# Weight scaling, low parts and partition copies moved to VectorE, q and k loaded ahead of the cap, and a new order, in an attention and gated-MLP kernel

## The chip, the cores and the metric

The kernel runs on one core of a Trainium2 chip. The metric is device time in microseconds: 728.2 us, the median of three runs (727.88 to 729.52). TensorE does the matrix products, VectorE (DVE), ScalarE (ACT) and GpSimd (POOL) the elementwise work, and SyncE (SP) issues the transfers.

## The reference, cut to what matters

```python
B, H, S, D = 8, 12, 448, 64                      # attention; DM = H*D = 768
scores = q @ k.T / sqrt(D);  scores = cap * tanh(scores / cap)
attn = exp(scores - max);    attn = attn / (attn.sum(-1) + 1e-9)
x = (attn @ v), heads joined to (B, S, 768)
h = relu(x @ w_in)                                # 768 x 1024
u, v = h[..., :512], h[..., 512:]
v_n = (v - mean(v)) / sqrt(var(v) + 1e-6)
v_s = w_spatial @ v_n (over the sequence) + b_spatial
out = (u * v_s) @ w_out                           # 512 x 768
```

All is float32; w_in and w_out come as float64 (the kernel reads their bits as pairs of 32-bit words).

## The kernel before, in words

The program has two variants behind a branch on the cap's value; with the cap of 30 the bounded one runs (`quad_bnd`, `moe`). In it no maximum is subtracted ahead of the exponential: exp(cap*tanh) is summed as it is, and the maximum enters only with the small constant of the denominator.

Attention goes in 24 turns (`quad_bnd`), three a batch, each of four heads. In a turn seven blocks of 64 keys are worked on. For each, TensorE makes the scores (L594), ScalarE the tanh out of PSUM (L598), then, over pairs of blocks, the exp (L605), and TensorE multiplies with v (L615). VectorE folds the exp tiles over the blocks for the maximum and, from the fourth turn on, for the sum (L633), transposes and reduces (L641, L643). In the first three turns TensorE makes the sums instead, by matmuls with ones (L662). Then the denominators: two copies between groups of 32 partitions (L649, tile `sh`), a join of both halves (L652, L679), in the first three turns DMAs that bring the sums to the tile `dt` (L674), a transpose, a reciprocal (L685), a round trip through DRAM that spreads the reciprocals over the partitions (L686, L689), and the multiplication (L698). `halves` splits the result into a rounded part and its rest, in the tile `xg`.

The MLP of a batch (`moe`) follows when its six `xg` tiles are there: chains of matmuls for u and v, the norm of v, the spatial product (L845 to L850) with the gate, and the output product. Each product takes three matmuls, high by high, high by low and low by high parts. So the weights have to be split once, in the first part of the program: `split_f64` for w_in (twelve pieces of 512 columns) and w_out (twelve of 256) takes six passes: a scaling (L420), three integer passes (L424, L425, L427), a rounding (L355) and the rest (L351), with the engines of the first, fifth and sixth in `E_W`. `split_f32` does w_spatial in four pieces, the last with the bias in two rows of the low part.

The order of all this is made when the program is built. `Plan.order` is a planner: it runs the tasks on a model of the engines, with the durations that each `add` names, and takes on each engine the ready task with the smallest key. The keys are made from `BND_KEY` and `BND_ADJ`, per kind and turn, and `BND_W_KEYS` for the weights. Buffers of one tag are also given in the order of the keys. `TURN` is what the planner charges when TensorE changes between the attention's and the MLP's kinds of matmul. Each engine then works in order, waiting on semaphores. The first MLP unit has `FILL` matmuls of weights by weights ahead of it, whose product is overwritten, and the program begins with `WARM` matmuls of zeros while the cap and the first q and k are loaded; the branch is decided by the cap, which all engines read.

Of the kernel before, what the change touches and what calls it, by code (L numbers as in the profile page):

```python
# [21 lines left out]
QB = 14  # L22
# [20 lines left out]
class Plan:  # L43
# [8 lines left out]
    TURN, STICK = 180.0, 5.6142  # L52
# [131 lines left out]
HW, HH, XL = 400, 620, 50  # L184
# [19 lines left out]
def dve(n):  # L204
    return 1.06 * n + 70
# [10 lines left out]
def gpc(n):  # L216
# [4 lines left out]
LATE = ("vh", "vl", "o")  # L221
# [4 lines left out]
    "xg": (XW, F32R, 8), "u": (448, F32, U_LEAD), "vh": (512, F32R, 4), "vl": (512, F32R, 4),  # L226
# [19 lines left out]
BND_KEY = dict(ld=20.2062, vld=16.3748, sc=-4.4101, th=2.6266, ex=-12.5751, pv=3.8334, sm=4.9568, mx=1.2536,  # L246
               dn=-1.9573, ev=0.5509, x=0.5743, moe=3.5126, span=11.5964, step=-1.1271, mv=-7.699, vld_=0.5863, sc_=0.1716,
               th_=0.234, ex_=3.1048, pv_=-0.3915, sm_=-0.1418, mx_=1.5249)
BND_ADJ = dict(sc0=-1.9208, sc1=-0.6751, sc2=-0.5665, sc3=0.6591, sc4=1.0022, sc5=0.9243, sc6=0.5641, sc7=3.5286,
               sc8=4.1291, sc9=2.1364, sc10=0.4432, sc11=-0.3562, sc21=1.0782, sc22=-2.0787, sc23=-1.8651, mx0=7.5468, mx1=4.1712,  # L250
               mx2=0.2306, mx3=-3.4986, mx4=-4.2501, mx5=-7.8699, mx6=-6.59, mx7=-4.2274, mx8=-1.6152, mx9=-1.0965, mx10=-2.503,
               mx11=2.4712, mx21=3.6487, mx22=7.5152, mx23=10.1101, sm0=-23.9232, sm1=-5.9121, sm2=-19.3382, sm3=-4.1068,
               sm4=-7.6692, sm5=-6.9113, sm6=-7.6076, sm7=-2.9296, sm8=-4.8786, sm9=-2.9017, sm10=0.1476, sm11=-1.028,
               sm21=7.8004, sm22=5.003, sm23=9.0892, dn0=-13.9326, dn1=2.5665, dn2=1.5054, dn3=3.678, dn4=5.4586, dn5=2.0101,
               dn6=-0.9345, dn7=1.341, dn8=5.2032, dn9=5.9753, dn10=6.5428, dn11=-0.3824, dn21=0.2627, dn22=-7.9155, dn23=32.9005,
               x0=-1.8155, x1=-12.9607, x2=-3.0392, x3=-3.3476, x4=1.7459, x5=0.4945, x6=3.9029, x7=6.1809, x8=0.3782, x9=6.0115,
# [698 lines left out]
```

## Time and profile before

| | |
|---|---|
| median of the runs | 728.2 us |
| profiled execution, its own time (given as the span alone) | 726.5 us |
| PE busy | 713.2 us (98%) |
| DVE busy | 600.4 us (83%) |
| ACT busy | 479.9 us (66%) |
| POOL busy | 78.4 us (11%) |

The page shows busy time by engine and, in forty slices, when it falls. A busy TensorE is not TensorE at its peak, since its matmuls overlap and their ends are modelled; the distance from one start to the next says more. The chain that ended last is 79% TensorE and 12% VectorE. Idle time of an engine that is not the bound costs nothing.

### The profile page before, as it was taken

To read this page: it belongs to the slowest core of one execution; us is meant where nothing else is said; L and a number is where in the kernel's file an instruction comes from. 1 tells how busy PE (TensorE), PEld (TensorE's weight loads), DVE (VectorE), ACT (ScalarE), POOL (GpSimd) and SP (SyncE) were. 2 spreads that over 40 slices of the span, in tenths; PEclk is the share of its full clock that TensorE was granted. 3 is DMA by queue.
4 is the path that set the end of the run, shared out by engine and by line. 5 is a ranking of instruction groups with operands and counts; after the bars stand their busy time and mean duration, and the time that the engine had idled before them with its cause. 6 is when DMAs were issued, how large, how long until landed. Compare 5 with 4: busy or idle time off the path is not lost.

```text
span 726.5 us, 12274 instructions
## 1 busy us (share of the span) xinstructions
PE 713.2 (98%) x4910; PEld 487.7 (67%) x4910; DVE 600.4 (83%) x849; ACT 479.9 (66%) x648; POOL 78.4 (11%) x71
## 2 busy tenths in 40 slices
PE   8998999999999999999999999999999999999997
PEld 3333576575668657785568688568566865699896
DVE  4899999999999989948999996299799778983520
ACT  6999757849883894649875833786876678424321
POOL 1234310600110001000120001000021000200100
PEclk9999999999999999999999999999999999999999
DMA  8564314524221431033321430124321131202002
GB/s 279 165 204 148 129 38 134 168 80 142 85 78 30 149 129 49 28 91 114 102 76 28 153 103 27 49 66 141 102 77 41 47 131 39 53 2 101 1 1 80
DMA packets 34263, 66.50 MB, mean 92 GB/s; under 512 B 6034, under 2 KB 21908, under 8 KB 34196
## 3 DMA queue, kind: packets, MB, share of 16 engines
q1 hardware_dynamic: 34196, 65.62, 28.3%
q8 instruction: 40, 0.66, 0.4%
q14 instruction: 27, 0.22, 0.1%
HBM read 54.40 MB, written 11.18 MB: 90 GB/s over the span
## 4 chain that ended last, share of the span: by engine, by line
PE 79%; DVE 12%; issue 4%; ACT 2%; DMA 1%; SPq 1%; POOL 0%; DVEq 0%; ACTq 0%; POOLq 0%
PE ps_s L594 13%; PE ps_x L615 13%; PE ps_acc L870 5%; PE ps_acc L871 5%; PE ps_acc L872 5%; PE ps_acc L754 4%; PE ps_acc L756 4%; PE ps_acc L755 4%; DVE red L633 4%; PE ps_acc L779 4%; PE ps_acc L780 3%; PE ps_acc L781 3%; PE ps_acc L848 2%; PE ps_acc L850 2%; PE ps_acc L849 2%
## 5 line engine op out<-in xcount | busy, mean ns | idle before, releaser
L598 ACT ACTIVATE tp<-ps_s,capt 128x896 f32<-128x896 f32 x168 | 162.2, 1003 | 28.6 <-PE ps_s L594 18.1
L633 DVE TENSOR_TENSOR red<-red,tp 128x1792 f32<-128x1792 f32 x90 | 140.9, 1566 | 22.5 <-ACT tp L605 20.8
L605 ACT ACTIVATE tp<-tp,capt 128x1792 f32<-128x1792 f32 (+1 forms) x96 | 154.0, 1606 | 1.5
L594 PE MATMUL ps_s<-raw 64*64 64x448 f32 x1344 | 147.1, 545 | 3.6 <-ACT tp L598 3.5
L615 PE MATMUL ps_x<-tp,v 64*64 64x448 f32 x1344 | 140.0, 536 | 0.5 <-ACT tp L605 0.4
L633 DVE TENSOR_TENSOR red<-tp 128x1792 f32<-128x1792 f32 x45 | 91.2, 2027 | 13.9 <-ACT tp L605 13.0
L615 PEld LDWEIGHTS ps_x<-tp,v 64*64 64x64 f32 x1344 | 51.3, 133 | 75.7 <-issue 68.2
L594 PEld LDWEIGHTS ps_s<-raw 64*64 64x64 f32 x1344 | 47.1, 132 | 80.1 <-issue 46.5
L803 POOL TENSOR_TENSOR lst<-lst,capt 128x1 f32<-128x1 f32 x32 | 34.9, 1091 | 526.7 <-DVE lst L801 482.9
L754 PE MATMUL ps_acc<-xg,wi_h 128*128 128x448 f32 x180 | 66.2, 368 | 0.5 <-ACT xg L355 0.5
L755 PE MATMUL ps_acc<-xg,wi_h 128*128 128x448 f32 x180 | 65.3, 363 | 0.7 <-DVE xg L351 0.6
L756 PE MATMUL ps_acc<-xg,wi_l 128*128 128x448 f32 x180 | 65.2, 362 | 0.0
L870 PE MATMUL ps_acc<-xg,wo_h 128*128 128x448 f32 x176 | 64.5, 367 | 0.0
L871 PE MATMUL ps_acc<-xg,wo_h 128*128 128x448 f32 x176 | 63.7, 362 | 0.6 <-DVE xg L351 0.6
L872 PE MATMUL ps_acc<-xg,wo_l 128*128 128x448 f32 x176 | 63.8, 362 | 0.0
L355 ACT CAST xg<-o 128x448 fp32r<-128x448 f32 x32 | 18.1, 566 | 55.0 <-DVE o L855 49.5
L641 DVE STREAM_TRANSPOSE red<-red 128x896 f32<-128x896 f32 x45 | 49.6, 1102 | 0.7
L779 PE MATMUL ps_acc<-wi_h,xg 128*128 128x512 f32 x126 | 50.1, 398 | 0.0
L643 DVE TENSOR_REDUCE st<-red 128x28 f32<-128x896 f32 x45 | 48.6, 1079 | 0.7
L780 PE MATMUL ps_acc<-wi_l,xg 128*128 128x512 f32 x126 | 49.1, 390 | 0.0
L781 PE MATMUL ps_acc<-wi_h,xg 128*128 128x512 f32 x126 | 49.1, 390 | 0.0
L633 DVE TENSOR_TENSOR red<-red 128x896 f32<-128x896 f32 x45 | 48.6, 1079 | 0.6
(146 smaller groups left out, 1110.1 us busy)
## 6 DMA issues: line engine op xcount, KB each, us to landing
raw<-in_qk SPq DMA_DIRECT2D x48, 448.0 KB
rr<-rd SPq DMA_DIRECT2D x48, 224.0 KB
out<-o SPq DMA_DIRECT2D x48, 224.0 KB
w<-in_w_in SPq DMA_DIRECT2D x12, 512.0 KB
v<-in_v SPq DMA_DIRECT2D x24, 256.0 KB
v<-in_v SPq DMA_DIRECT2D x24, 192.0 KB
xg<-in_w_out SPq DMA_DIRECT2D x12, 256.0 KB
rd<-dt SPq DMA_DIRECT2D x48, 3.5 KB
```

Of the source, the lines that this page charges most:

```text
L594: nc.tensor.matmul(ps.t[c * D:(c + 1) * D, e, :S], lhsT=f(raw[c].t)[r, k:k + D], rhs=f(raw[c].t)[r, :S], start=True, stop=True)
L598: th = add("A", act(PW, 1), kk("th", i), lambda ps=ps, tp=tp, o=o: nc.scalar.activation(out=tp.t[:, o:o + PW].rearrange("p (e q) -> p e q" ...
L605: ex = add("A", act_s(w, 1), kk("ex", i), lambda tp=tp, w=w: nc.scalar.activation(out=tp.t[:, :w], in_=tp.t[:, :w], func=AF.Exp, scale=ca) ...
L615: nc.tensor.matmul(x.t[e * D:(e + 1) * D, c, :S], lhsT=vts[g // 2].t[c * D:(c + 1) * D, (4 * (g % 2) + 2 * j + e) * D:(4 * (g % 2) + 2 * j ...
L633: nc.vector.tensor_tensor(o_(), i0(), i1(), op=op)
L754: nc.tensor.matmul(ps, lhsT=wi1_h[:, c, fs], rhs=x[:, XH:], start=(c == 0), stop=False)
L755: nc.tensor.matmul(ps, lhsT=wi1_h[:, c, fs], rhs=x[:, :S], start=False, stop=False)
L756: nc.tensor.matmul(ps, lhsT=wi1_l[:, c, fs], rhs=x[:, XH:], start=False, stop=(c == NP - 1))
L779: nc.tensor.matmul(ps, lhsT=x[:, XH:][:, ts], rhs=wi2_h[:, c], start=(c == 0), stop=False)
L870: nc.tensor.matmul(ps, lhsT=wo_h[:, c, ns], rhs=g[:, XH:], start=(c == 0), stop=False)
L871: nc.tensor.matmul(ps, lhsT=wo_h[:, c, ns], rhs=g[:, :S], start=False, stop=False)
L872: nc.tensor.matmul(ps, lhsT=wo_l[:, c, ns], rhs=g[:, XH:], start=False, stop=(c == 3))
```

## The change

- `E_W` goes from `"PAV"` to `"VAV"`: the scaling of the 24 weight pieces is done on VectorE.
- In `split_f32` the low parts are made on VectorE; the bias, in rows that the host now repeats, comes in one DMA and one copy, with no clearing.
- The two copies between groups of partitions (`sh`) are made on VectorE.
- The sums of the first three turns go to `dt` by two DMAs in place of four.
- The cap is loaded from ScalarE's queue, so that the two loads of q and k are SyncE's first.
- The last tile of the normalised v has a buffer of its own (`vht`), and its row of ones is written once, for the first batch alone.
- `WARM` goes from 14 to 11; the planner's `TURN` from 180 to 120, some durations and nearly all keys are new.

```diff
@@ -49,7 +49,7 @@
-    TURN, STICK = 180.0, 5.6142
+    TURN, STICK = 120.0, 5.6142
@@ -181,7 +181,7 @@
-HW, HH, XL = 400, 620, 50
+HW, HH, HD, XL = 400, 620, 900, 50
@@ -202,7 +202,7 @@
-    return 1.06 * n + 70
+    return 1.04 * n + 70
@@ -218,12 +218,12 @@
-LATE = ("vh", "vl", "o")
+LATE = ("vh", "vl", "o", "vht")
...
-    "xg": (XW, F32R, 8), "u": (448, F32, U_LEAD), "vh": (512, F32R, 4), "vl": (512, F32R, 4),
+    "xg": (XW, F32R, 8), "u": (448, F32, U_LEAD), "vh": (512, F32R, 3), "vht": (512, F32R, 1), "vl": (512, F32R, 4),
@@ -243,28 +243,35 @@
-BND_KEY = dict(ld=20.2062, vld=16.3748, sc=-4.4101, th=2.6266, ex=-12.5751, pv=3.8334, sm=4.9568, mx=1.2536,
-               dn=-1.9573, ev=0.5509, x=0.5743, moe=3.5126, span=11.5964, step=-1.1271, mv=-7.699, vld_=0.5863, sc_=0.1716,
...
-BND_ADJ = dict(sc0=-1.9208, sc1=-0.6751, sc2=-0.5665, sc3=0.6591, sc4=1.0022, sc5=0.9243, sc6=0.5641, sc7=3.5286,
...
-               dn6=-0.9345, dn7=1.341, dn8=5.2032, dn9=5.9753, dn10=6.5428, dn11=-0.3824, dn21=0.2627, dn22=-7.9155, dn23=32.9005,
-               x0=-1.8155, x1=-12.9607, x2=-3.0392, x3=-3.3476, x4=1.7459, x5=0.4945, x6=3.9029, x7=6.1809, x8=0.3782, x9=6.0115,
...
+BND_KEY = dict(ld=44.0117, vld=11.782, sc=-4.3696, th=12.5403, ex=-10.8391, pv=6.0377, sm=3.9021, mx=1.6556, dn=-6.9308,
+               ev=4.1189, x=2.4802, moe=4.2989, span=10.6921, step=-0.5386, mv=-10.0916, vld_=-0.2079, sc_=0.1515, th_=0.0803,
...
+BND_ADJ = dict(sc0=-17.0128, sc1=-10.2479, sc2=-6.3835, sc3=-5.1053, sc4=1.3971, sc5=-0.4773, sc6=-2.5798, sc7=0.152, sc8=6.4698,
...
+               sm19=8.3808, sm20=5.6527, sm21=9.214, sm22=9.6274, sm23=21.5531, dn0=-13.1225, dn1=-10.3538, dn2=-10.2789,
...
+               dn20=-0.904, dn21=4.5003, dn22=-5.8298, dn23=-0.9526, x0=-20.4935, x1=-32.2365, x2=-21.7903, x3=-7.9643,
...
-WARM, WARM_N, FILL = 14, 512, 8
-BND_W_KEYS = -14.6272, 0.1578, -3.1507, 14.803, -4.1788, 0.5729, 0.2535
+WARM, WARM_N, FILL = 11, 512, 8
+BND_W_KEYS = -19.1639, -2.2043, 3.2534, 12.2756, -3.6568, -5.836, 3.1289
...
-E_W = "PAV"
+E_W = "VAV"
@@ -293,13 +300,14 @@
-        if b.tag in TAGS or b.tag in EARLY:
+            own["vht"] = [pools["vht"].tile([128, 512], F32R, name="vht")]
+        if b.tag in own:
+            b.t = own[b.tag].pop(0)
+        elif b.tag in TAGS or b.tag in EARLY:
...
-        elif b.tag in own:
-            b.t = own[b.tag].pop(0)
@@ -374,28 +382,16 @@
-        rows = slice(c * 128, c * 128 + n)
+        rows = slice(c * 128, (c + 1) * 128)
...
-        a = add("S", HW, key, lambda: load(t.t[:n, :S], rows), allocs=[t], lat=dm(n, 4 * S))
+        a = add("S", HW, key, lambda: load(t.t[:, :S], rows), allocs=[t], lat=dm(128, 4 * S))
+        b = add("V", dve2(S), key, lambda: nc.vector.tensor_copy(hi, t.t[:, :S]), [a], [t])
+        l = [add("V", dve(S), key, lambda: sub("V", lo[:n], t.t[:n, :S], f(hi[:n])), [b], [t], name="ws")]
...
-            a = add("S", HW, key, lambda: load(t.t[n:, :S], rows), [a], [t], lat=dm(n, 4 * S))
-        b = add("V", dve2(S), key, lambda: nc.vector.tensor_copy(hi, t.t[:, :S]), [a], [t])
-        l = [add("P", gp(S), key, lambda: sub("P", lo[:n], t.t[:n, :S], f(hi[:n])), [b], [t])]
-        if c == 3:
-            y = Buf("wy")
-
-            def bias():
-                for i in (64, 96):
-                    load(y.t[i:i + 1, :S], slice(S, S + 1))
-
-            def parts():
-                nc.vector.memset(f(lo[64:]), 0.0)
-                for i in (64, 96):
-                    nc.vector.tensor_copy(lo[i:i + 1], y.t[i:i + 1, :S])
-                sub("V", lo[96:97], y.t[96:97, :S], f(lo[96:97]))
-
-            a = add("S", 2 * HW, key, bias, [], [y], [y], lat=XL)
-            l.append(add("V", 1500, key, parts, [a], [y]))
+            y, some = Buf("wy"), slice(D, 97)
+            a = add("S", HW, key, lambda: load(y.t[some, :S], slice(512, 545)), [], [y], [y], lat=XL)
+            a = add("V", dve2(S), key, lambda: nc.vector.tensor_copy(lo[some], y.t[some, :S]), [a], [y], name="ws")
+            l.append(add("V", dve(S), key, lambda: sub("V", lo[96:97], y.t[96:97, :S], f(lo[96:97])), [a], [y], name="ws"))
@@ -618,7 +614,7 @@
-        z = add("A", act(PW, 1), kk("ev"), lambda: nc.scalar.copy(out=two(xf.t), in_=x.t[:, :, :S]), [prev], [x, xf], [xf], name="xev")
+        z = add("A", act(PW), kk("ev"), lambda: nc.scalar.copy(out=two(xf.t), in_=x.t[:, :, :S]), [prev], [x, xf], [xf], name="xev")
@@ -646,7 +642,7 @@
-            d = [add("A", 145, kk("dn"), lambda p=p, o=o: nc.scalar.copy(out=sh.t[p, :32 * len(done)], in_=st.t[o, :32 * len(done)]), d,
+            d = [add("V", 110, kk("dn"), lambda p=p, o=o: nc.vector.tensor_copy(sh.t[p, :32 * len(done)], st.t[o, :32 * len(done)]), d,
@@ -670,10 +666,9 @@
-                for e in range(2):
-                    outs.append(add("S", HW, kk("dn"), lambda c=c, e=e: nc.sync.dma_start(
-                        out=dt.t[64 * c + e * QB:64 * c + (e + 1) * QB, 32:64],
-                        in_=sxs[c].t[D * e:D * e + 1].rearrange("p (b i) -> p b i", i=32)), [q, room], [sxs[c], dt], lat=dm(QB, 128)))
+                outs.append(add("S", HD, kk("dn"), lambda c=c: nc.sync.dma_start(
+                    out=dt.t[64 * c:64 * c + n1, 32:64],
+                    in_=sxs[c].t[0:128:64].rearrange("p (b i) -> p b i", i=32)), [q, room], [sxs[c], dt], lat=dm(n1, 128)))
@@ -765,8 +760,9 @@
-                acc, vr, ls, vh, vl = Buf(next(tags)), Buf("stg"), Buf("lst"), Buf("vh"), Buf("vl")
-                ts, last = slice(t * 128, (t + 1) * 128), t == 3
+                last = t == 3
+                acc, vr, ls, vh, vl = Buf(next(tags)), Buf("stg"), Buf("lst"), Buf("vht" if last else "vh"), Buf("vl")
+                ts = slice(t * 128, (t + 1) * 128)
@@ -813,9 +809,9 @@
-                    s5 = add("V", 541, kv(k), ones, late, [vh], [vh], name="ones")
+                    s5 = add("V", 680, kv(k), ones, late, [vh], [vh], name="ones") if b == 0 else None
...
-                             name="vnh")
+                             [] if b == 0 else [vh], name="vnh")
@@ -898,7 +894,7 @@
-    nc.sync.dma_start(out=capt[:, 0:1], in_=args[4].broadcast_to([128, 1]))
+    nc.scalar.dma_start(out=capt[:, 0:1], in_=args[4].broadcast_to([128, 1]))
@@ -935,7 +931,8 @@
-    ws = np.concatenate([moe_w_spatial.T[order], moe_b_spatial.reshape(1, S)], axis=0)[:, order]
+    wt, bias = moe_w_spatial.T[order], moe_b_spatial.reshape(1, S)
+    ws = np.concatenate([wt, wt[384:], bias, np.zeros((31, S), np.float32), bias], axis=0)[:, order]
```

## Rows read from the trace of the kernel before

**Rows 1.** The page: its first line, and busy us by engine.

```profile
span 726.5 us, 12274 instructions
...
PE 713.2 (98%) x4910; PEld 487.7 (67%) x4910; DVE 600.4 (83%) x849; ACT 479.9 (66%) x648; POOL 78.4 (11%) x71
```

**Rows 2.** Stretches of 25 us: busy us of PE, PEld, DVE, ACT, POOL; clock, DMA.

```profile
0.00:25.00 25.00, 22.36 (x187) 8.84 (x190) 14.56 (x22) 18.45 (x19) 5.62 (x16) 1.00 0.80 273
25.00:50.00 25.00, 24.62 (x260) 9.11 (x256) 22.05 (x32) 23.87 (x28) 5.26 (x5) 1.00 0.50 154
50.00:75.00 25.00, 20.84 (x168) 8.71 (x166) 24.39 (x40) 24.24 (x35) 12.68 (x5) 0.93 0.56 183
75.00:100.00 25.00, 25.00 (x165) 17.24 (x164) 24.35 (x31) 16.25 (x21) 5.37 (x2) 1.00 0.24 72
```

**Rows 3.** Timeline, TensorE, 61 to 74 us: start, us, what.

```profile
61.72 1.68 PE L594 MATMUL ps_s<-raw 64*64 64x448 f32 x16
...
66.29 2.62 PE L594 MATMUL ps_s<-raw 64*64 64x448 f32 x16 [2.89 <-ACT tp L598]
...
72.10 0.47 PE L754 MATMUL ps_acc<-xg,wi_h 128*128 128x448 f32 x1 [0.52 <-ACT xg L355]
...
73.52 0.36 PE L756 MATMUL ps_acc<-xg,wi_l 128*128 128x448 f32 x1
```

**Rows 4.** Chain that ended last, 161 to 166 us: start, us, what.

```profile
161.98 0.20 PE ps_acc L872
...
162.78 0.91 PE ps_s L594 x8
163.70 1.50 PE ps_x L615 x16
```

**Rows 5.** Timeline, the first 7 us, SyncE and TensorE.

```profile
1.17 0.90 SPq L904 DMA_DIRECT2D raw<-in_qk  x2
...
1.17 5.49 PE L910 MATMUL wps<-warm 128*128 128x512 bf16 x14 [1.17 <-DVE capt L913]
...
4.90 1.29 SPq L413 DMA_DIRECT2D w<-in_w_in  x3
...
6.77 1.73 PE L594 MATMUL ps_s<-raw 64*64 64x448 f32 x16
```

**Rows 6.** Groups of VectorE by shape, to 90 us: busy us, mean ns.

```profile
L425 DVE SCALAR_TENSOR_TENSOR wy<-w,wy 128x512 uint32<-128x512 uint32 x12 | 9.0, 756 | 0.1
...
L633 DVE TENSOR_TENSOR red<-red,tp 128x896 f32<-128x896 f32 x4 | 5.3, 1322 | 0.1
...
L424 DVE TENSOR_SCALAR wy<-wy 128x512 uint32<-128x512 uint32 x12 | 4.8, 414 | 5.5 <-POOL wy L420 5.5
...
L633 DVE TENSOR_TENSOR red<-red 128x896 f32<-128x896 f32 x4 | 4.3, 1068 | 0.0
...
L394 DVE CAST ws_l<-wy 1x448 fp32r<-1x448 f32 x2 | 1.4, 698 | 0.1
```

**Rows 7.** Timelines of ScalarE, SyncE and VectorE, 49 to 69 us.

```profile
49.83 0.22 ACT L649 COPY sh<-st 32x32 f32<-32x32 f32 x1
...
52.52 0.21 ACT L649 COPY sh<-st 32x32 f32<-32x32 f32 x1
...
52.45 2.87 SPq L674 DMA_DIRECT2D dt<-u  x3
...
55.53 0.17 DVE L652 TENSOR_TENSOR st<-st,sh 96x28 f32<-96x28 f32 x1
...
68.52 1.15 DVE L698 TENSOR_TENSOR xf<-xf,rr 128x448 f32<-128x448 f32 x2
```

**Rows 8.** One tile, w: its L425 passes, ns min/median/max.

```profile
L425 DVE SCALAR_TENSOR_TENSOR wy<-w,wy x12: 669/692/1520, 9.6 to 83.4; 128x512 uint32<-128x512 uint32 x12
```

**Rows 9.** Timelines of POOL and VectorE.

```profile
51.29 9.14 POOL L351 TENSOR_TENSOR ws_l<-wy,ws_h 128x448 fp32r<-128x448 f32 x1 [3.24 <-DVE ws_h L382]
...
9.14 0.43 DVE L424 TENSOR_SCALAR wy<-wy 128x512 uint32<-128x512 uint32 x1 [4.92 <-POOL wy L420]
```

More of the change, by code (lines that the diff above doesn't have):

```diff
@@ L245 @@
 ANY_W_KEYS = 2, 0.5, 8, 9, 1, 5, 0.5
-BND_KEY = dict(ld=20.2062, vld=16.3748, sc=-4.4101, th=2.6266, ex=-12.5751, pv=3.8334, sm=4.9568, mx=1.2536,
-               dn=-1.9573, ev=0.5509, x=0.5743, moe=3.5126, span=11.5964, step=-1.1271, mv=-7.699, vld_=0.5863, sc_=0.1716,
-               th_=0.234, ex_=3.1048, pv_=-0.3915, sm_=-0.1418, mx_=1.5249)
-BND_ADJ = dict(sc0=-1.9208, sc1=-0.6751, sc2=-0.5665, sc3=0.6591, sc4=1.0022, sc5=0.9243, sc6=0.5641, sc7=3.5286,
[L250 to L254, printed above, removed]
-               dn6=-0.9345, dn7=1.341, dn8=5.2032, dn9=5.9753, dn10=6.5428, dn11=-0.3824, dn21=0.2627, dn22=-7.9155, dn23=32.9005,
-               x0=-1.8155, x1=-12.9607, x2=-3.0392, x3=-3.3476, x4=1.7459, x5=0.4945, x6=3.9029, x7=6.1809, x8=0.3782, x9=6.0115,
-               x10=5.0057, x11=0.7894, x21=7.5672, x22=-1.7504, x23=1.6104, moe0=-2.1731, moe1=4.7513, moe2=2.8101, moe3=2.4916,
-               moe7=9.0071, span0=-2.667, span1=-3.3859, span2=-2.449, span3=-5.6885, span7=28.8127, mv0=4.9503, mv1=-2.4788,
-               mv2=2.6326, mv3=3.2084, mv7=-12.8989, wi0=-3.2806, wi1=-21.6066, wi2=-37.6263, wi3=14.5167, wi4=16.5614,
-               wi5=1.1376, wi6=13.0344, wi7=2.468, wi8=-18.9783, wi9=3.3202, wi10=-13.2504, wi11=-12.154, ws0=-12.654,
-               ws1=-7.9959, ws2=-33.2129, ws3=-10.2049, wo0=-6.4452, wo1=-0.8201, wo2=2.6051, wo3=8.6589)
```

18 lines of the change are left out of this document (added).

## The prediction

> **What bounds the kernel now.** I read the page first, then the table of 25 us stretches, then TensorE's timeline around the stretch that stood out, then the timelines of the engines that fed it. The reader is to see in the page that TensorE is busy for 713.2 of 726.5 us [rows 1]: in the whole, only work taken off TensorE or holes in its stream can shorten the kernel, and the change takes none off. The table by stretches says where the holes are: 22.36 of the first 25 us, 24.62 of the second, 20.84 of the third [rows 2]; the one after them is full. VectorE is the reverse: 14.56, 22.05, then 24.39 of 25; and ScalarE, with 23.87 and 24.24 in the second and third, is as full.
>
> The hole that counts is near 65 us. The score matmuls that start at 61.72 end at 63.40; the next sixteen wait 2.89 us and start at 66.29, then come eight filler matmuls that compute nothing (FILL), the first of the MoE at 72.10, and a regular stream only from 73.52 [rows 3]. In these 10.1 us the useful work is sixteen attention matmuls, 1.5 us at full rate, and three of the MoE, at 0.20 each [rows 4]. So 8.0 us are lost here. The granted clock averages 0.93 over the stretch from 50 to 75 us [rows 2], so part of the loss is a spell at the lower level after TensorE had starved; it goes with the starving and has no term of its own.
>
> Two lesser losses: the start, with the first score at 6.77 us right behind the end of the warm-up at 6.66 [rows 5], and each passage from MoE to attention, whose first eight matmuls take 0.91 us in the chain where sixteen in stride take 1.50, that is 0.16 us [rows 4].
>
> The profiled execution is given only as its span, 726.5 us; the median of the timed runs is 728.2. I work in differences against the span and let the 1.7 us around it stand.
>
> **The change part by part.**
>
> *Start: q and k ahead of the cap, eleven warm-ups.* The cap's load was issued on SyncE before the two loads of q and k; the branch that it decides lets SyncE issue its first weight load at 4.90 [rows 5]. Fourteen warm-ups take 5.49 us, 0.39 each; three fewer let TensorE go 1.2 us earlier, at 5.5. ScalarE issues the cap's load now, and has little else to do until the scores. If the cap's tiny packets get behind those of q and k, I charge 0.90 us, what the two loads took to issue [rows 5], as the nearest price: the branch then comes at 5.8 and the first score at about 5.9. I take that, a gain of 0.8 us. Bounds: a gain of 1.2 (the cap is not delayed), and a loss of 0.5 (the cap lands after all of q and k, the branch some two us late, with first scores near 7.3).
>
> *Weight scaling on VectorE (twelve pieces of 512 columns before 85 us, twelve of 256 after).* The nearest row is the other one-input pass over the same tile, 414 ns x12 [rows 6]: +5.0 us of VectorE work, in the front of the program. *Low parts of the spatial weights* (four): half of a clean 896-column combination, 1.07 us [rows 6], so 0.55 each, +2.2. *Bias rows*: two one-row casts of 698 ns [rows 6], a clear and a SyncE load become one cast and one load: -1.0. *Partition copies*: forty-eight ScalarE copies, of 0.21 to 0.22 us where they are 32 columns wide [rows 7], become VectorE copies; the nearest VectorE row is a 96x28 combination, 0.17 [rows 7], so 0.2 each and six in the front: +1.2. Sum, +7.4 us.
>
> Against this stands what POOL costs VectorE when both work. The twelve L425 passes average 756 ns where their median is 692, the worst 1520 [rows 6, 8]: 0.8 us, and L427, a pass over the same tile, as much. The narrow combinations that read a new tile average 1322 where the plain ones take 1068 [rows 6]: 4 x 0.25 = 1.0. With a few others below 0.3 each I take 3 us back. Net, VectorE gets 4.4 us more before 85 us. Its cover is its own idle time: 2.95 us from 25 to 50, and from its late beginning at 9.14 [rows 9] to 25 about 2 (15.86 us, of which it is busy for all but some 0.7 of its 14.56) [rows 2]. Of 5.0 us the 4.4 just fit; whatever does not fit falls into the stretch where VectorE has 0.6 us free, straight into the hole.
>
> *What POOL's queue did.* One low part of the spatial weights, begun at 51.29, took 9.14 us on POOL, and three scalings of w_in stood behind it until 60.43 [rows 9]. On VectorE these pieces can no longer be held up by another engine. I give this no term of its own: VectorE was busy throughout, so it only frees the choice of what to do first.
>
> *The chain that opens the MoE.* Here the change cuts latency. The first MoE unit waits for attention outputs of the second turn, and so do those of the first turn: both take their xg buffers in the order of the keys, and x1 makes the second turn's -7.8 and the first's -1.2 (the new ones, -25.8 and -18.0, keep that order). Its maximum was ready at 49.83, when ScalarE made the first partition copy; the second came at 52.52, behind an exp and a cast, and VectorE joined the two at 55.53 only [rows 7]. With the copies on VectorE that join can come at 49.8 + 2 x 0.2, up to 5 us earlier. The sums go to their place by four SyncE DMAs, of which the last three took 2.87 us from 52.45, to 55.3 [rows 7]; two of the new kind, at 0.96 each from about 50.2, when the maximum has freed the place, end at 52.1, 3.2 us earlier. Both must be in before the reciprocal, its round trip through DRAM, and the multiplication at 68.52 [rows 7]. The later of the two sets it: 3 to 5 us earlier, so I take 4.0 off the hole's 8.0 (ScalarE's six copies less, 1.3 us, are in it). After that the casts and weight pieces still on ScalarE and VectorE are what is late next. Bounds: 8.0 gained (the hole is gone); 4.4 lost (VectorE's added work has no cover).
>
> The Trainium skill has a rule that speaks against the copies: in "VectorE: DVE Perf Modes", section "Two Vector instructions with no wait between them", an instruction that starts in another group of 32 partitions than the one before it is held until all earlier ones have finished. The bias casts, which go to partitions 64 and 96, took 698 ns for 448 columns where L424 takes 414 for 512 [rows 6], which fits it, though POOL worked beside them. By that difference, 0.3 us, six copies would cost 1.8 us more in the front, and the sum below would be 725.2.
>
> *ones once instead of eight times, output weights' scaling, ScalarE's relief.* Seven clears go and twelve 256-column scalings come to VectorE; ScalarE loses forty-eight copies. All but the first few lie behind 75 us, where TensorE's stretch is full [rows 2] because attention and MoE of different batches cover each other; 0. If that cover fails around 100 to 165 us, twelve scalings at the price of L424 at most, 5.0 us, less what POOL gives back, cost about 2; a gain there is at most 1.
>
> *Order anew, a turn priced at 120 ns in place of 180.* The keys are new for nearly every task. From the trace before I can't lay out the new order. A cheaper turn in the planner's sum lets it change more often between attention and MoE; six turns more or fewer at 0.16 to 0.35 us (the 0.16 above plus as much on the way back) are 1 to 2 us either way. I take 0. *The single row of the last v tile (vht)* takes a buffer from the four of vh; a batch has four v tiles, one of them this one, so each batch finds as many as before: 0.
>
> Sum: 726.5 - 0.8 - 4.0 = 721.7 in the span, 723.4 us in the median.
>
> **The rivals.**
>
> *The hole closes (719).* If the x chain gains its 5 us and the weights are put early enough into VectorE's idle 5 us, TensorE goes from attention into the MoE with a rest of a microsecond: 0.8 + 7 + 1 from smoother stretches to 165 us, 719.4. For: both waits of the chain are touched at once, and POOL's queue is gone. Against: ScalarE is also full there, and the tile buffers still hold attention back.
>
> *Nothing but the start (727.4).* The x chain is earlier, but the weights are not: the last three w_in pieces end when VectorE has done all its work, and that sum hardly changes. Then only 0.8 us are gained. For: VectorE is busy for 24.39 of 25 us there [rows 2]. Against: pieces of the last tiles of w_in are wanted only by later units.
>
> *VectorE becomes the bound of the front (slower, 731.8).* Place: 10 to 85 us. Price: its net 4.4 us, if the idle time before 50 us can't be used because the weights' three buffers or their loads are not there, land in the hole; the start's 0.8 comes off. 728.2 + 4.4 - 0.8 = 731.8. It decides from the point where less than about half of the added work finds idle time, since the chain's 4 us are then eaten too (each reduction that waits holds a score buffer, and ScalarE and TensorE wait with it). For: the shown idle time is only 5.0 us. Against: POOL's hold on VectorE falls away at the same time.
>
> **How the numbers follow.** The forecast, with its own range of 721 to 726, gets 0.50; the closed hole 0.17; the start alone 0.17; VectorE as the bound 0.16. This kernel's three runs lie within 1.6 us, so 0.2%, or 1.5 us, is about what a measurement can tell from no change: 726.7 to 729.7. The forecast and the closed hole are faster; of the start alone 0.05 is; the rest of it, 0.12, is within; a little of the slow case, 0.02, too. Faster 0.72, same 0.14, slower 0.14. The range of 717 to 730 leaves out some 0.05 below (hole, start and turns all at their best) and 0.12 above.
>
> **What would show it.** Start: first score at 5.5 to 6.0 us, the first weight load before 6. Scaling: POOL's list ends at the powers of the norms; L425 and L427 without outliers above 0.8. Chain: the partition copies within 0.5 us behind the maximum, the sums' DMAs two per turn, the second turn's multiplication before 66 us. Hole: TensorE's 50 to 75 us stretch at 23 or more. Wrong would be: first scores after 7 us; VectorE's partition copies at half a microsecond; the same hole moved to another place; or more passages between attention and MoE with new waits behind them.

## The result and the profile after

The changed kernel takes 734.7 us in the median (733.6 to 735.2), beside 728.2 before: a ratio of 1.0082, interval 1.007 to 1.0094. By the medians it is 6.5 us slower, where a gain of 4.8 us was forecast. Its profiled execution has a span of 732.8 us. The page, busy us by engine, answers to [rows 1]:

```profile
span 732.8 us, 12196 instructions
...
PE 714.3 (97%) x4907; PEld 485.9 (66%) x4907; DVE 613.3 (84%) x916; ACT 468.7 (64%) x600; POOL 24.8 (3%) x43
```

TensorE has as much to do as before; VectorE has 12.9 us more, ScalarE 11.2 less, POOL 53.6 less. The stretches of 25 us, in the columns of [rows 2]:

```profile
0.00:25.00 25.00, 21.00 (x171) 7.64 (x175) 15.21 (x30) 17.06 (x18) 0.84 (x11) 1.00 0.79 280
25.00:50.00 25.00, 23.57 (x248) 8.76 (x244) 24.72 (x48) 23.18 (x27) 0.00 (x0) 1.00 0.61 196
50.00:75.00 25.00, 20.75 (x196) 6.85 (x188) 24.75 (x34) 24.68 (x25) 0.00 (x0) 0.93 0.47 150
75.00:100.00 25.00, 23.23 (x163) 14.37 (x164) 24.61 (x38) 20.69 (x31) 0.00 (x0) 1.00 0.27 85
```

All four of TensorE's numbers are lower than in [rows 2], and the hole now reaches past 75 us. VectorE's idle time from 25 to 50 us, 2.95 us before, is nearly used up.

The first 16 us (timelines of the queues, VectorE and TensorE; answers to [rows 5]):

```profile
0.73 0.39 ACTq L897 DMA_DIRECT2D capt<-in_cap  x1
0.74 0.88 SPq L900 DMA_DIRECT2D raw<-in_qk  x2
...
5.09 0.15 DVE L908 TENSOR_SCALAR capt<-capt 128x1 uint32<-128x1 uint32 x1 [3.96 <-DMA capt<-in_cap]
...
6.16 2.24 PE L590 MATMUL ps_s<-raw 64*64 64x448 f32 x16
6.28 1.28 SPq L409 DMA_DIRECT2D w<-in_w_in  x3
7.67 1.06 SPq L579 DMA_DIRECT2D v<-in_v  x2
...
15.48 1.73 PE L611 MATMUL ps_x<-tp,v 64*64 64x448 f32 x16 [1.36 <-DMA v<-in_v]
```

The first score comes 0.61 us earlier than 6.77, but the sixteen take 2.24 us in place of 1.73, so they end only 0.10 us earlier. The cap reaches VectorE at 5.09; in the kernel before it did at 3.69:

```profile
3.69 0.15 DVE L912 TENSOR_SCALAR capt<-capt 128x1 uint32<-128x1 uint32 x1 [2.56 <-DMA capt<-in_cap]
```

So the branch is decided later, and the first loads of weights go out at 6.28 in place of 4.90, those of v behind them. TensorE has the scores early and then waits 1.36 us for v.

TensorE around the hole (answers to [rows 3]; L590 are scores, L748 fillers, L749 to L751 the MoE):

```profile
64.07 1.68 PE L590 MATMUL ps_s<-raw 64*64 64x448 f32 x16
...
67.93 3.27 PE L590 MATMUL ps_s<-raw 64*64 64x448 f32 x16 [2.18 <-ACT tp L594]
71.92 1.88 PE L590 MATMUL ps_s<-raw 64*64 64x448 f32 x16 [0.73 <-ACT tp L594]
76.32 1.88 PE L590 MATMUL ps_s<-raw 64*64 64x448 f32 x16 [2.52 <-ACT tp L594]
78.13 1.89 PE L748 MATMUL ps_acc<-wi_h 128*128 128x448 f32 x8
...
80.66 0.47 PE L750 MATMUL ps_acc<-xg,wi_h 128*128 128x448 f32 x1 [0.45 <-DVE xg L359]
80.97 0.36 PE L751 MATMUL ps_acc<-xg,wi_l 128*128 128x448 f32 x1
```

The steady stream of the MoE begins at 80.97 (73.52 before). More attention is done ahead of it (608 of its matmuls in place of 576), but at the pace of ScalarE's tanh (L594), with three waits where there was one.

Where the time went, worked out from the trace's matmuls: T less the matmuls begun by T, each at its full-rate time (0.094 us for the quarter-array ones, 0.200 for 448 columns, 0.226 for 512; warm-ups and fillers count nothing). It is what TensorE has lost up to T, in us. The labels are those of the experiments below.

```
lost up to T =                  15     60     80    200    450    700
before                         8.6   10.4   19.2   24.7   28.6   32.0
after                          9.7   12.6   22.6   27.5   33.4   37.8
e1_start_undone                8.6   11.1   21.8   26.2   32.3   36.0
e2_old_order_new_engines       8.2   10.7   22.7   29.4   35.0   38.4
e7_only_copies                 8.2   11.5   22.3   28.6   33.8   37.2
e9_moves_fill_16               8.2   10.4   19.9   28.6   34.0   37.4
e10_after_copies_back          9.0   11.5   22.8   28.1   33.4   37.0
e11_small_edits_old_order      9.0    9.6   18.8   23.6   27.4   30.8
e17_new_order_nine_folds_less  8.2   10.4   20.8   24.0   29.6   33.4
e18_before_nine_folds_less     8.2    8.9   19.5   23.2   27.0   30.2
```

Of the 5.8 us that the change loses by 700 us, 2.2 come before 60 us (half by 15 us: the start), 1.2 in the hole, and 3.0 after 200 us, where the forecast had nothing; between 80 and 200 us 0.6 come back. Each row is one execution: e7 and e16 (below) are the same program up to 100 us, and at 80 us they lie 1.2 us apart. So a microsecond at one point of one row proves little.

### The profile page after: what moved, and what is told of

Its sections match the earlier page's. It is cut to its first block, busy times and chain, and to the rows that moved or that the text cites. A ratio compares the mean times of both kernels' runs of the same rounds, so it can differ in the third digit from the quotient of the medians.

```text
span 732.8 us, 12196 instructions
## 1 busy us (share of the span) xinstructions
PE 714.3 (97%) x4907; PEld 485.9 (66%) x4907; DVE 613.3 (84%) x916; ACT 468.7 (64%) x600; POOL 24.8 (3%) x43
## 4 chain that ended last, share of the span: by engine, by line
PE 76%; DVE 15%; ACT 4%; DMA 2%; issue 2%; SPq 0%; DVEq 0%; ACTq 0%
PE ps_x L611 13%; PE ps_s L590 12%; DVE red L629 5%; PE ps_acc L866 4%; PE ps_acc L749 4%; PE ps_acc L751 4%; PE ps_acc L750 4%; PE ps_acc L867 4%; PE ps_acc L868 4%; PE ps_acc L775 3%; PE ps_acc L776 3%; PE ps_acc L777 3%; PE ps_acc L844 2%; PE ps_acc L846 2%; PE ps_acc L845 2%
## 5 line engine op out<-in xcount | busy, mean ns | idle before, releaser
L594 ACT ACTIVATE tp<-ps_s,capt 128x896 f32<-128x896 f32 x168 | 163.3, 1007 | 25.5 <-PE ps_s L590 22.7
L590 PE MATMUL ps_s<-raw 64*64 64x448 f32 x1344 | 149.1, 548 | 7.8 <-ACT tp L594 7.7
L601 ACT ACTIVATE tp<-tp,capt 128x1792 f32<-128x1792 f32 x96 | 154.0, 1608 | 1.4
L590 PEld LDWEIGHTS ps_s<-raw 64*64 64x64 f32 x1344 | 47.4, 133 | 86.1 <-issue 49.4
L749 PE MATMUL ps_acc<-xg,wi_h 128*128 128x448 f32 x180 | 66.2, 368 | 0.0
L751 PE MATMUL ps_acc<-xg,wi_l 128*128 128x448 f32 x180 | 65.2, 362 | 0.0
L799 POOL TENSOR_TENSOR lst<-lst,capt 128x1 f32<-128x1 f32 x32 | 23.9, 747 | 663.8 <-DVE lst L797 662.2
```

The source lines that it names most:

```text
L590: nc.tensor.matmul(ps.t[c * D:(c + 1) * D, e, :S], lhsT=f(raw[c].t)[r, k:k + D], rhs=f(raw[c].t)[r, :S], start=True, stop=True)
L594: th = add("A", act(PW, 1), kk("th", i), lambda ps=ps, tp=tp, o=o: nc.scalar.activation(out=tp.t[:, o:o + PW].rearrange("p (e q) -> p e q" ...
L601: ex = add("A", act_s(w, 1), kk("ex", i), lambda tp=tp, w=w: nc.scalar.activation(out=tp.t[:, :w], in_=tp.t[:, :w], func=AF.Exp, scale=ca) ...
L749: nc.tensor.matmul(ps, lhsT=wi1_h[:, c, fs], rhs=x[:, XH:], start=(c == 0), stop=False)
L751: nc.tensor.matmul(ps, lhsT=wi1_l[:, c, fs], rhs=x[:, XH:], start=False, stop=(c == NP - 1))
```

## Experiments

Ratios are against the kernel before on the same chip (medians 729.0 to 729.5 us), with 95% intervals. "Frozen order" means that the order of issue on each engine is kept and only the named instruction goes to another engine or is left out.

### The start: e1 and e4

e1 is the changed kernel with the cap first on SyncE and fourteen warm-ups; e4 the kernel before with the changed start alone.

```diff
-WARM, WARM_N, FILL = 11, 512, 8
+WARM, WARM_N, FILL = 14, 512, 8
-    nc.scalar.dma_start(out=capt[:, 0:1], ...)
+    nc.sync.dma_start(out=capt[:, 0:1], ...)
```

> The changed kernel with the start of before: the cap's load first on SyncE again, 14 warm-ups; everything else, the order too, as changed. Three theories on the 6.5 us that the change lost. Start: the cap lands 1.4 us later (5.09 against 3.69 us), so the first loads of w_in and v are issued 1.4 us later (6.28 against 4.90), TensorE waits 1.4 us for v and VectorE begins later; then this run gains 1.5 to 3 us: 731.7 to 733.2. VectorE: its added work in a front where it is full is the loss; then this run gains at most 1 us: 733.7 to 734.7. Order: the new keys are the loss; the same 733.7 to 734.7.

> The kernel before with the changed start alone: the cap's load on ScalarE's queue, q and k first on SyncE, 11 warm-ups; the order is that of before. Start: the first scores come 0.6 us earlier, but w_in and v 1.4 us later, so 1 to 2 us slower than before: 729.2 to 730.2. VectorE and order: the start is worth little either way, 727.5 to 728.7. The prediction's own step: 0.8 us faster, 727.4.

e1: 733.7 us, 1.0067 (1.0053 to 1.008). e4: 730.0, 1.0011 (1.0002 to 1.0021). The start costs about 1 us in either kernel (in the changed one the intervals with and without it overlap); forecast was a gain of 0.8. Some 5 us of loss are elsewhere, as two of e1's three theories had it.

### Engines or order: e2 and e3

e2 is the kernel before, frozen, with scalings, spatial low parts and copies on VectorE. e3 is the changed kernel, frozen, with these on POOL and ScalarE again.

```diff
-  eng[E_W[0]].tensor_scalar(yf(), i, 2.0 ** -112, ...)
+  eng["V"].tensor_scalar(yf(), i, 2.0 ** -112, ...)
-  sub("P", lo[:n], t.t[:n, :S], f(hi[:n]))
+  sub("V", lo[:n], t.t[:n, :S], f(hi[:n]))
-  nc.scalar.copy(out=sh.t[p, ...], in_=st.t[o, ...])
+  nc.vector.tensor_copy(sh.t[p, ...], st.t[o, ...])
```

> The kernel before, planned as before, so that every engine's program has its order, but the scaling of the weights, the low parts of the spatial weights and the partition copies are issued on VectorE at their old places. VectorE: its programme gets the 24 scalings, 4 low parts and 48 copies in a front where it is full, so 4 to 6 us slower than before: 732 to 734. Order: the engines alone don't matter, within 1.5 us of before: 727 to 729.5. Start: the same as order.

> The changed kernel, planned as changed, so that every engine's program has the new order, but the weights' scaling and the spatial weights' low parts are issued on POOL and the partition copies on ScalarE, as before. VectorE: with the work off it most of the loss is gone: 729 to 731. Order: no better than the changed kernel, since the order is kept: 733.5 to 738 (POOL's waits come on top). Start: as the changed kernel, 734 to 735.

e2: 735.85, 1.0093 (1.0078 to 1.0109). e3: 738.1, 1.0116 (1.01 to 1.0133). The moves alone cost 6.9 us in the old order, as much as the whole change and more than the 4 to 6 of e2's theory. The old order with the new engines (e2) and the new order with them (1.0067 without the start) can't be told apart for certain: e1 also has the small edits, which are worth about 0.1% beyond the low parts (e11 against e8 below). e3 came out slow, as the order theory had it, and not at 729 to 731: with the old engines the new order has no advantage left.

### Which of the moves: e6, e7, e8

> The kernel before with its order of issue; only the 24 weight scalings (L420) issued on VectorE in place of POOL: by their times in the changed kernel 4.8 us before 85 us and 3.4 us after. Theory (VectorE's added work before 85 us goes into the end, all three moves together cost 6.9 us): the scalings carry most of it, +3 to +5 us, 731 to 734. Rival (the partition copies, queued behind folds on VectorE, carry it): the scalings alone within 1 us of before, 728 to 730.

> The kernel before with its order of issue; only the 48 partition copies (L649) issued on VectorE in place of ScalarE: 0.17 to 0.19 us each, 1.1 us of it before 85 us. Theory (VectorE's load is what costs): within 1 us of before, 728 to 730, since ScalarE is relieved by 1.3 us in the same stretch. Rival (the copies queue behind 2 us folds on VectorE, and the sums and the attention output behind them come later in each of the 24 turns): +3 to +6 us, 731 to 735, spread over the whole span.

> The kernel before with its order of issue; only the four low parts of the spatial weights issued on VectorE in place of POOL: 0.6 us each, 2.4 us. Theory (VectorE's load is what costs): +1 to +2.4 us, 729.5 to 731. Rival (POOL held VectorE while it did the 9.14 us piece, and its queue held three scalings up): the same or faster, 727 to 729.

Each is one of e2's three edits. Scalings: 730.7, 1.0016 (0.9997 to 1.0034). Copies: 734.1, 1.0065 (1.0048 to 1.0082). Low parts: 728.7, 0.9991 (0.998 to 1.0003). So 8.2 us of scaling cost about 1 us, not clear of nothing; the low parts cost nothing; and the copies, 9.1 us of which only 1.0 is ahead of 85 us, cost 4.7. My theories for all three missed; the rivals held for the copies and the low parts, and nearly for the scalings. The parts add up to 5.3 of e2's 6.9 us; the rest is not explained. TensorE in e7, the hole:

```profile
66.60 1.88 PE L594 MATMUL ps_s<-raw 64*64 64x448 f32 x16 [2.17 <-ACT tp L598]
68.41 1.89 PE L753 MATMUL ps_acc<-wi_h 128*128 128x448 f32 x8
72.86 0.74 PE L754 MATMUL ps_acc<-xg,wi_h 128*128 128x448 f32 x1 [2.56 <-ACT xg L355]
...
75.22 0.57 PE L754 MATMUL ps_acc<-xg,wi_h 128*128 128x448 f32 x1
75.60 0.57 PE L755 MATMUL ps_acc<-xg,wi_h 128*128 128x448 f32 x1
```

The MoE opens 0.76 us later than at 72.10 [rows 3], and its matmuls then start 0.37 apart in place of 0.20. VectorE's multiplication of the second turn starts at 70.30, in the kernel before at 68.52 [rows 7]. POOL and VectorE of e7 (the low part of [rows 9] is the first row):

```profile
51.19 1.51 POOL L351 TENSOR_TENSOR ws_l<-wy,ws_h 128x448 fp32r<-128x448 f32 x1 [3.54 <-DVE ws_h L382]
52.79 0.98 POOL L420 TENSOR_SCALAR wy<-w 128x512 f32<-128x512 f32 x1
...
51.62 1.63 DVE L425 SCALAR_TENSOR_TENSOR wy<-w,wy 128x512 uint32<-128x512 uint32 x1
53.17 2.47 DVE L633 TENSOR_TENSOR red<-tp 128x1792 f32<-128x1792 f32 x1
55.68 0.18 DVE L649 COPY sh<-st 32x32 f32<-32x32 f32 x1
55.89 0.69 DVE L351 TENSOR_TENSOR wi_l<-wy,wi_h 128x512 fp32r<-128x512 f32 x1
```

POOL's piece took 9.14 us before, beside a VectorE that ran on; here it takes 1.51, and VectorE's pass beside it 1.63 in place of 0.68; the fold, beside POOL's next piece, takes 2.47 in place of 2.02. But the copies are not the reason. e13 (below), which leaves them out, shows the same:

```profile
51.30 1.52 POOL L351 TENSOR_TENSOR ws_l<-wy,ws_h 128x448 fp32r<-128x448 f32 x1 [3.26 <-DVE ws_h L382]
...
51.73 1.63 DVE L425 SCALAR_TENSOR_TENSOR wy<-w,wy 128x512 uint32<-128x512 uint32 x1
```

Its multiplication starts at 69.45, so 0.9 of e7's 1.8 us of delay come without any copy, and its MoE opens at 72.20, at no loss. The copy itself: in e7 the fold ends at 55.64 and the next pass starts at 55.89, where two passes in a row overlap by 0.08. Over all 48 copies the median is 0.25 + 0.08 = 0.32 us of VectorE for a copy that its row gives as 0.18.

### The clock: e9

e2 with sixteen fillers in place of eight ahead of the first of the MoE.

```diff
-WARM, WARM_N, FILL = 14, 512, 8
+WARM, WARM_N, FILL = 14, 512, 16
```

> The kernel before with its order of issue and the three moves to VectorE (735.85 us when run before), with sixteen filler matmuls in place of eight ahead of the first of the MoE. In that run the fillers ended at 71.1, the first of the MoE came at 73.06, and TensorE then ran at the lower clock until 79.9: fourteen matmuls at 0.37 apart in place of 0.20, 2.4 us. Theory (the pause behind the fillers brings the lower clock down on useful work): with the pause filled the clock stays up, and 1.5 to 2.4 us come back, 733.4 to 734.4. Rival (the fall of the clock comes from the hole before, whatever fills the pause): no gain, 735.5 to 736.5.

734.7, 1.0077 (1.0058 to 1.0096). From 72 to 80 us (windows; first e2, then e9):

```profile
72.00:80.00 8.00, 6.04 (x16) 5.05 (x17) 8.00 (x14) 7.09 (x12) 0.00 (x0) 0.58 0.56 210
```

```profile
72.00:80.00 8.00, 6.65 (x38) 4.93 (x40) 8.00 (x13) 6.76 (x11) 0.00 (x0) 1.00 0.55 201
```

With the pause filled the clock is 1.00 instead of 0.58, and 38 matmuls are begun instead of 16. By 80 us 2.8 us are won; by 200 us 2.0 of them are lost again, the intervals of e2 and e9 overlap, and the time lies between theory and rival. In e9 (as in e2 and e7) the longest wait from 80 to 200 us is this one:

```profile
146.15 3.24 PE L615 MATMUL ps_x<-tp,v 64*64 64x448 f32 x32 [1.93 <-ACT xf L621]
```

It is 0.6 us longer than in e2 (1.32). A TensorE that is early meets here what ScalarE has not done yet; for the other 1.4 us I can't name the waits.

### VectorE's load taken away: e5, e14, e16

Without the second fold of the maximum (2.02 us) in some turns; the third piece of the scores then stays out of the maximum.

```diff
-  lambda rw=rw, fold=fold: fold(rw, rw, lambda: tps[2].t)
+  lambda ..., skip=(a == 0 and turn < 4): None if skip else fold(rw, rw, lambda: tps[2].t)
```

> The changed kernel with its order of issue, without the second fold of the maximum (L629, 2.02 us each) in the first four turns: the third piece of the scores stays out of the maximum of those turns. 8.1 us of VectorE work go from the stretch of 20 to 90 us, and nothing else. Theory (VectorE's work before 85 us has no cover, so it sets TensorE's holes there): most of the 8.1 us comes back, 4 to 7 us against the changed kernel's 734.7, so 728 to 731. Rival (the order of issue and the latency of single chains set the holes, VectorE has room): under 1.5 us, 733.2 to 734.7.

> The changed kernel with its order of issue, without the second fold of the maximum (L629, 2.02 us) in turns 4 to 8, between 100 and 200 us: 10.1 us of VectorE work go there; the third piece of the scores stays out of the maximum of those turns. Theory (from 85 to 200 us VectorE is full and sets the end, where the front to 80 us was set by ScalarE and the chain): 2 to 4 us back, 730.5 to 732.7. Rival (there too it has room for TensorE's needs): under 1 us, 733.7 to 734.7.

> The kernel before with its order of issue and the copies on VectorE (734.06 us when run before), without the second fold of the maximum (L633, 2.02 us) in turns 4 to 8, between 100 and 200 us. Theory (VectorE's time up to 200 us is what the copies cost): 3 to 5 us back, 729 to 731. Rival (the loss at 60 to 80 us, 2.9 us with the lower clock, is lost for good): at most 1.5 us back, 732.5 to 734.

e5: 733.4, 1.0057 (1.0037 to 1.0077). e14: 734.0, 1.0065 (1.0048 to 1.0082). e16: 731.45, 1.003 (1.002 to 1.0041). My theories for e5 and e14 missed, and the rivals' times held: 8 or 10 us off VectorE give back 1 to 2. The stretch from 65 to 75 us says why (first after, then e5):

```profile
65.00:75.00 10.00, 5.90 (x40) 1.10 (x32) 9.87 (x15) 10.00 (x11) 0.00 (x0) 0.83 0.43 139
```

```profile
65.00:75.00 10.00, 6.19 (x36) 1.26 (x32) 7.21 (x12) 10.00 (x12) 0.00 (x0) 0.67 0.47 141
```

VectorE gets 2.7 us of idle time, ScalarE stays full, and TensorE still waits for ScalarE's tanh. In e16 2.5 us of the copies' 4.7 come back, between the two theories; 1.2 of them are there by 80 us, ahead of the folds left out, so they can't be put down to these. In e16 the lower clock fell on scores and fillers (granted 0.59 from 68 to 72 us, 1.00 from 72 to 80), in e7 on the MoE (0.57 from 72 to 80).

### The copies elsewhere or nowhere: e10, e13, e15

> The changed kernel with the start undone (733.7 us when run before) and its order of issue; the 48 partition copies issued on ScalarE again. Theory (the copies cost on VectorE in any order, 4.9 us by the run with them alone): 3 to 5 us come back, 728.7 to 730.7. Rival (the new order was laid out with the copies on VectorE, and ScalarE is busy for 10.00 of 10 us from 65 to 75): no gain or a loss, 733 to 736.

> The kernel before with its order of issue, the 48 partition copies left out (the maximum and the sum across partitions then miss parts). Theory (on ScalarE they cost nothing, since ScalarE has idle time there after 75 us and the chain's latency was not what set the hole): 728 to 729.5, beside 729.2 with them. Rival (the latency of the copies sets the opening of the MoE, as the prediction had it): 3 to 5 us faster, 724 to 726.

> The kernel with the small edits in the old order (727.5 us when run before), the 48 partition copies issued on POOL, which is idle for most of the span: neither ScalarE nor VectorE has them. Theory (what the copies cost is VectorE's time): as that kernel or a little faster, 726.5 to 728. Rival (they cost by standing in another engine's queue and by the handing over, whatever the engine): 730 to 733.

e10: 732.7, 1.0045 (1.0027 to 1.0062). e13: 728.1, 0.9988 (0.9978 to 0.9997). e15: 728.6, 0.9988 (0.9979 to 0.9998). The copies cost about 1 us on ScalarE, and e13's rival, which is the prediction's own step (their latency sets the opening of the MoE, 3 to 5 us), falls. On POOL, where they take longest, they cost some 0.5 us more than on ScalarE (e15 against e11), which the intervals don't separate from nothing; the time lies a little above the theory's range and far below the rival's. On VectorE they cost 5.6 (0.0065 + 0.0012). The groups of e15 and e7 (busy us, mean ns):

```profile
L649 POOL COPY sh<-st 32x64 f32<-32x64 f32 (+1 forms) x48 | 40.3, 844 | 308.7 <-DVE st L643 291.4 <-DVE lst L801 16.1
```

```profile
L649 DVE COPY sh<-st 32x64 f32<-32x64 f32 (+1 forms) x48 | 9.1, 194 | 1.4
```

A copy of 844 ns on an idle engine is cheaper than one of 194 ns on a full one: it is VectorE's time and order that cost, not the copy's own duration. In the new order 1 to 2 us come back with the copies on ScalarE, less than the theory's 3 to 5: that order was laid out for them on VectorE.

### The small edits and the order: e11, e12, e17, e18

e11 is the kernel before, frozen, with the low parts on VectorE, one load and one cast for the bias rows, and two sum loads in place of four. e12 is the changed kernel with the old keys, price of a turn and start. e17 (on e1) and e18 (on before) lack the second folds of turns 0 to 8.

```diff
-  load(y.t[i:i + 1, :S], slice(S, S + 1))          # i = 64, 96
+  load(y.t[64:97, :S], slice(512, 545))
-  out=dt.t[64 * c + e * QB:64 * c + (e + 1) * QB, 32:64]   # e = 0, 1
+  out=dt.t[64 * c:64 * c + n1, 32:64]
```

> The kernel before with its order of issue and the edits that add nothing to VectorE but the spatial low parts: these on VectorE, the bias rows by one load and one cast, the sums of a turn by two loads into place in place of four. Theory (these take latency and work off the chain that opens the MoE, and put 2.4 us on VectorE against 1.0 off): 0.5 to 1.5 us faster than before, 727.5 to 728.5 beside 729.0. Rival (the chain is not set by the sums): as the spatial low parts alone, 728.5 to 729.2.

> The changed kernel with its engines and small edits, its order planned anew with the keys and the price of a turn of the kernel before, and the start of the kernel before. Theory (the moves cost 5 to 7 us whatever the order, since VectorE is full before 85 us): 732 to 736. Rival (the cost lies in issuing the moved work where an order made for other engines put it, and a planner that knows the engines hides it): 727 to 730.

> The changed kernel with the start undone (733.7 us when run before) and its order of issue, without the second fold of the maximum (2.02 us) in turns 0 to 8: 18.2 us of VectorE's work go before 215 us; the third piece of the scores stays out of the maximum of those turns. Theory (the new order keeps ScalarE full in the hole and makes six more passages between attention and MoE, whatever VectorE does): 731 to 732.5, the sum of what the four and the five folds gave. Rival (VectorE's load is the cause): 727 to 729.5.

> The kernel before with its order of issue, without the same nine folds. Theory (there VectorE's load sets little beyond the small waits): 0 to 2 us faster than before, 727.5 to 729.5 beside 729.3. Rival (VectorE sets the end there as well): 3 us or more faster, under 726.5.

e11: 727.5, 0.9981 (0.9971 to 0.9991): faster than both kernels, and the version to keep. e12: 753.1, 1.0319 (1.0299 to 1.034): far outside both of its ranges. e17: 730.5, 1.0022 (1.0011 to 1.0032). e18: 726.2, 0.9955 (0.9941 to 0.9969). Taking 18.2 us off VectorE helps the two orders alike: from 1.0067 to 1.0022 and from 1 to 0.9955. The gap between them stays at 0.67%. So VectorE's load costs both some 3.3 us (e18's rival held; e17 lies between its two), and does not explain why one is slower; the new order with its engines does, and these two runs don't part order from engines. TensorE's waits in e17, with VectorE at 6.42 of 10 us from 65 to 75 (waits: total us, times, longest; e18 has 3.3 in 2 of this kind):

```profile
PE ps_s L590 <- ACT tp L594: 6.0, 7, 2.2
```

e12 shows how much can lie in the order: new engines under old keys take 24 us more than before; 9 of them are lost by 100 us.

## Why the prediction was wrong

The sum was -0.8 for the start, -4.0 for the chain, and 0 for the moves to VectorE and for the order. Measured are about +1.0 for the start, +6.9 for the moves in the old order (e2), and +4.9 for moves, chain edits and new order together (e1).

**What bounds the kernel: right for TensorE and the hole, wrong in how far VectorE mattered.** I read 75 us as the end of the front. From 50 us on VectorE stays busy for 24.35 to 25.00 of each 25 us until 200, and 0.65% came from forty-eight copies most of which lie behind 85 us.

**Start, -0.8: wrong in sign, about +1.0 (e1, e4).** The 0.90 that I charged for the cap's delay was 1.40 (3.69 to 5.09), and the branch that waits for it also holds back the loads of weights and v. I counted the first score and not the second wait. The Trainium skill, "DMA: Bandwidth & Descriptors", section "Issuing engines are not separate DMA queues", says that transfers started by ScalarE and SyncE run on the same sixteen engines and interleave; the later landing beside q and k agrees.

**Engine moves, "of 5.0 us the 4.4 just fit", 0: the largest failure.** In e2 they cost 6.9 us, with 4.7 from the copies by themselves. The instruction prices were near: scaling 0.42 (0.414 forecast), low parts 0.6 (0.55), copies 0.17 to 0.19 (0.2). Two things were not in the sum. A copy takes 0.32 us of VectorE's time. And with a VectorE that was late by one or two microseconds at the opening of the MoE, the lower clock fell onto useful work in e2 and e7, some 2.4 us; in the changed kernel it fell on scores (the sixteen of 67.93 took 3.27 us). POOL, the rival cause, held VectorE up in e7, but as much in e13, which lost nothing. From the Trainium skill, "VectorE: DVE Perf Modes", section "Two Vector instructions with no wait between them", on instructions that start in another group of 32 partitions, I made a rival sum with 0.3 us a copy. It held in kind, at half the price: measured are 0.14 us beyond the copy's own time.

**"All but the first few lie behind 75 us: 0": wrong.** From 200 to 700 us before loses 7.3 us, e7 8.6, e1 9.8. This repeats: the old order with no copies on VectorE (e4, e6, e8, e11, e13, e15, e18) loses 6.9 to 7.8 there, with them (e2, e7, e9, e16) 8.4 to 9.0, and the new order with them (after, e1, e5, e14, e17) 9.4 to 10.3. I had left out that ScalarE's queue, in order, stands behind VectorE. The clearest case is at 145 us in e7. The cast of 144.91 begins 0.07 us after VectorE's last pass over an xg buffer (144.43 to 144.84); the profile names no releaser, so this link is read from the times. Behind it comes the eviction at 145.81, for which TensorE waits 1.57 us. In the kernel before the same cast (141.88) finds VectorE done and does not wait; first e7, then before:

```profile
144.91 0.57 ACT L355 CAST xg<-o 128x448 fp32r<-128x448 f32 x1 [1.47 <-issue]
...
145.81 0.91 ACT L621 COPY xf<-ps_x 128x896 f32<-128x896 f32 x1
```

```profile
141.88 0.56 ACT L355 CAST xg<-o 128x448 fp32r<-128x448 f32 x1
...
142.76 0.91 ACT L621 COPY xf<-ps_x 128x896 f32<-128x896 f32 x1
```

**Chain, -4.0: wrong; neither the copies nor the sums' loads set it.** The second turn's chain on VectorE of the changed kernel (answers to [rows 7]):

```profile
58.52 1.07 DVE L639 TENSOR_REDUCE st<-red 128x28 f32<-128x896 f32 x1
...
60.22 0.17 DVE L645 COPY sh<-st 32x32 f32<-32x32 f32 x1
60.42 2.02 DVE L629 TENSOR_TENSOR red<-tp 128x1792 f32<-128x1792 f32 x1
62.48 0.18 DVE L645 COPY sh<-st 32x32 f32<-32x32 f32 x1
62.68 2.03 DVE L629 TENSOR_TENSOR red<-red,tp 128x1792 f32<-128x1792 f32 x1
64.63 0.18 DVE L648 TENSOR_TENSOR st<-st,sh 96x28 f32<-96x28 f32 x1
...
76.76 1.15 DVE L693 TENSOR_TENSOR xf<-xf,rr 128x448 f32<-128x448 f32 x2
```

The maximum is ready at 59.59, 10 us later than before, and the multiplication comes at 76.76 (68.52 before). The new order puts weights ahead of attention on VectorE: by 50 us it has done one of the integer passes (L425, in the changed kernel L421) for ten pieces instead of five, and one maximum instead of two (groups to 50 us, first before, then after; e1, with the old start, has the same counts):

```profile
L425 DVE SCALAR_TENSOR_TENSOR wy<-w,wy 128x512 uint32<-128x512 uint32 x5 | 4.3, 856 | 0.1
L643 DVE TENSOR_REDUCE st<-red 128x28 f32<-128x896 f32 x2 | 2.2, 1086 | 0.1
```

```profile
L421 DVE SCALAR_TENSOR_TENSOR wy<-w,wy 128x512 uint32<-128x512 uint32 x10 | 6.8, 687 | 0.1
L639 DVE TENSOR_REDUCE st<-red 128x28 f32<-128x896 f32 x1 | 1.1, 1079 | 0.0
```

Between the maximum and the join lie two folds, 5.0 us: I had put the copies back to back, and a copy stands in VectorE's queue as it stood in ScalarE's. In the old order (e11) the two sum loads end at 52.20 in place of 55.3, the 3 us of the forecast, but the multiplication starts only 0.76 us earlier (67.76), and the maximum itself 1.3. Without any copy (e13) it is not earlier either (69.45). In the kernel before, VectorE shows no wait between the maximum and 70.2 us, past the multiplication: it was full with folds and weight passes, as the prediction itself read (0.6 us free). So it waited for neither copies nor loads, and the 4.0 could come only from an order that puts this chain ahead of them. e11 gains 1.4 us in all (0.9981), and which of its edits brings it was not tested apart.

**Order and turns, 0: wrong.** Without its start the new order with its engines costs 0.67% with VectorE loaded and with VectorE relieved (e17, e18). Two of the prediction's signs of being wrong are there: the hole has moved, and there are 57 passages between attention and MoE in place of 51. In the hole it is ScalarE's pace that the trace shows. After 175 us there are 42 passages between attention and MoE in place of 39, at the 0.35 us I gave them at most 1 us of e1's 2.5 us there; copies back on ScalarE (e10) take 0.9 of these. Which key or task makes the rest stays open, and so does how the 4.9 us of e1 divide between the order and the engines: the copies are 1.6 of them (e10), the other 3.3 were not parted.

**The rivals.** "VectorE becomes the bound of the front", 731.8, is nearest in time, but by luck: 8.1 us less of VectorE in the front gave 1.3 to 1.8 (e5), so its mechanism carries a small part at most, and of the 5.8 us only 3.4 are lost by 80 us.

## What to carry to other kernels

Before a small operation is moved to an engine that is full over a long stretch, count it at its start-to-start price and ask which in-order queues wait for that engine's results: here 48 copies of 0.18 us cost 5 us, and on an idle engine four times slower some 1 to 1.5. An order made by tuned keys belongs to its engines: test an edit in the frozen order, where its own worth shows, before a new order is made around it. When a load is put earlier, look at what the delayed one releases, not only at who uses the early one.

## What the runs showed of the hardware

VectorE and POOL hold each other up, and who gets in changes from kernel to kernel: the same POOL piece took 9.14 us and VectorE lost nothing in the kernel before (8.99 in e6, 5.30 in e4), or it took 1.51 and VectorE's pass beside it lost 0.95, the fold beside POOL's next piece 0.46 (e7; the same in e13, e16 and e18). What decides it was not tested; copies on VectorE don't, since e13 and e18 have none. The Trainium skill, "SBUF — State Buffer", section "Who interferes with whom", calls the pair of ports that they share an exclusive lock; both cases agree, with the holder exchanged.

TensorE's clock falls from 2.4 to 1.2 GHz for some microseconds after the starving near 65 to 72 us, at a moment that small delays move. In the kernel before, the granted clock was 0.66 from 68 to 72 us and 1.00 from 72 to 80: the spell lay on scores and fillers inside the hole (the eight fillers took 2.74 us, in e7 1.89) and had ended when the first of the MoE was ready at 72.10. In e2 and e7 a pause of 2.0 and 2.6 us followed the fillers, and a spell lay on the first fourteen or so matmuls of the MoE: 14 x 0.17, some 2.4 us. With eight more fillers (e9) the clock was 1.00 there; one kernel does not tell a rule from chance, since e16 kept its MoE at 1.00 with eight fillers and a pause of 1.1 us.
